# Attention and two expert layers on one core: 64-bit weights decoded with a parametric ReLU, one shift and an integer addition; every low part of the activation on VectorE

## The chip, the cores and the metric

The kernel runs on one core of a Trainium2 chip. The metric is device time in microseconds (us) of one execution. The profile is a separate execution of the same program. Engine names as in the profile: PE is TensorE's matmul (PEld its weight load), DVE is VectorE, ACT is ScalarE, POOL is GpSimd, SP is the queue that issues DMAs.

## The reference

Three stages follow one another: attention restricted to clusters, a dense layer with a rational activation (called the first layer here), and eight experts weighted by a balanced gate (the second layer).

```python
attn = softmax over k of (scale * q @ k.T where cluster(q) == cluster(k))     # B=2, H=8, S=768, D=64
x = (attn @ v), heads side by side                                            # 1536 x 512
h = x @ w_in                                                                  # w_in 512 x 2048, 64-bit floats
P = a[0] + a[1]*h + a[2]*h**2 + a[3]*h**3
Q = 1.0 + abs(b[0])*abs(h) + abs(b[1])*h**2
x = (P / (Q + 1e-6)) @ w_out                                                  # w_out 2048 x 512, 64-bit floats
gate = exp(x @ w_gate - max), rows and columns normalised 8 times             # 1536 x 8
out = sum over e of gate[:, e] * (relu(x @ w1[e]) @ w2[e])                    # w1 8 x 512 x 1024, 32-bit
```

The weights of the first layer arrive as 64-bit floats, all others as 32-bit.

## The kernel before, in words

Every matmul operand is kept as a high part (rounded for TensorE, tile names ending in h: `wh`, `hh`, `XH`) and a low part (what the rounding left: `wl`, `hl`, `XL`). A product is three matmuls: high by high, high by low, low by high (`mm3`, L784 to L786).

The first layer is cut into 8 units of 256 hidden columns. A unit has two weight pieces, `i = 0` (a slice of `w_in`) and `i = 1` (a slice of `w_out`). It is worked in 6 steps, one for each of three chunks of 512 tokens and two groups of 128 columns: 48 steps in all. In a step TensorE makes 12 matmuls for one 128x512 block of h (`stage1`) and 12 for two blocks of the output (`stage2`), four steps later.

The activation of step n is spread over the engines. ScalarE reads h from PSUM four times (`act_b`, L825 to L828), GpSimd does two multiply-adds for the numerator (L829, L830), VectorE the denominator (`act_q`, L834), ScalarE the logarithm and the exponential of its negative, which is the reciprocal (`act_r`, L838, L842). One step later VectorE makes the high part `hh` (L848), two helper values (L849, L852) and the low part `hl` (L855). In every third step from n = 6 the low part is made by GpSimd instead (L853), with a copy of the reciprocal in SBUF that a second exponential writes (L841); there are 14 such steps. VectorE also adds the output blocks to the accumulator (L887; the first unit's are copied by ScalarE, L885).

A 64-bit weight is read as two 32-bit words, `lo` and `hi`. `split_w` decodes a piece of 128x1024 weights in six pieces of work, one in each of six consecutive steps (`step_a` to `step_f`), into `wh` and `wl`: two on ScalarE (L654, L665), four on VectorE (L657, L660, L666, L667), two on GpSimd (L670, L673). There are 16 such decodings, one every three steps; those of unit 0, and the first piece of unit 1, begin while the last pair of attention heads is still at work. The 32-bit weights of the second layer take another path (`plain`, L641, L642), which is not touched.

The order on each engine is the order in which the program's loop writes the instructions (the loop from L1204); no scheduler moves them. Within a step the loop writes `act_b`, then the accumulator additions mixed with the activation's VectorE work and the pieces of decoding (L1213 to L1223), then `act_r`, `stage1`, `stage2`, and last the first piece of a new decoding. `stage1` has three PSUM buffers, so its matmuls of step n+3 wait for the last reader of h of step n, which is the low part.

Of the kernel before, what the change touches and what calls it, by code (L numbers as in the profile page):

```python
# [9 lines left out]
F32 = mybir.dt.float32  # L10
# [3 lines left out]
AF = mybir.ActivationFunctionType  # L14
ALU = mybir.AluOpType
# [15 lines left out]
def kernel(  # L31
# [15 lines left out]
    nc = tc.nc  # L47
# [69 lines left out]
    gt = nc.gpsimd.tensor_tensor  # L117
# [47 lines left out]
    lnb = const.tile([P, 2], F32, name="lnb")  # L165
# [461 lines left out]
    def split_w(ui, i):  # L627

        if (ui, i) not in staged:
            return []  # L630
        raw = staged.pop((ui, i))
        shape = [P, *wshape[i]]
        wh, wl = weights[ui, i] = (
            wp.tile(shape, F32R, tag=f"wh{i}", name=f"wh_{ui}_{i}"),
            wp.tile(shape, F32R, tag=f"wl{i}", name=f"wl_{ui}_{i}"),
        )
        if units[ui][0] == 1:

            def plain(h):
                c = slice(h * wshape[i][0] // 2, (h + 1) * wshape[i][0] // 2)  # L640
                nc.gpsimd.tensor_scalar(wh[:, c], raw[:, c], 1.0, 1.0, op0=ALU.mult, op1=ALU.mult)  # L641
                gt(wl[:, c], raw[:, c], wh[:, c].bitcast(F32), op=ALU.subtract)  # L642

            return [lambda: plain(0), lambda: plain(1)]

        lo, hi = raw[..., 0], raw[..., 1]
        mag = dp.tile(shape, F32, tag="mag", name=f"mag_{ui}_{i}")
        top = dp.tile(shape, F32, tag="top", name=f"top_{ui}_{i}")  # L650
        mi, ti = mag.bitcast(U32), top.bitcast(U32)

        def step_a():
            nc.scalar.activation(mag, hi.bitcast(F32), AF.Copy, scale=2.0 ** -112)  # L654

        def step_b():
            nc.vector.tensor_scalar(mi, mi, 3, None, op0=ALU.logical_shift_left)  # L657

        def step_c():
            nc.vector.scalar_tensor_tensor(  # L660
                ti, hi, 0x80000000, mi, op0=ALU.bitwise_and, op1=ALU.bitwise_or
            )

        def step_d():
            nc.scalar.copy(wh, top)  # L665
            nc.vector.tensor_scalar(mi, ti, 0xFF800000, None, op0=ALU.bitwise_and)  # L666
            nc.vector.scalar_tensor_tensor(mag, lo, 2.0 ** -52, mag, op0=ALU.mult, op1=ALU.mult)  # L667

        def step_e():
            gt(top, top, wh.bitcast(F32), op=ALU.subtract)  # L670

        def step_f():
            gt(wl, top, mag, op=ALU.add)  # L673

        return [step_a, step_b, step_c, step_d, step_e, step_f]

    B0, B1, B2 = 8, 14, 20
    LASTK = 2 * NT * (NPR - 1)
# [2 lines left out]
    def begin(x, ui, i):  # L681
        for y, fn in enumerate(split_w(ui, i)):
            early.setdefault(x + y, []).append(fn)

    mctx = ctx.enter_context(ExitStack())
    for kk in attention():
        if kk == LASTK:
            pctx.close()
            wp = left("wp", 2)
            stg = mctx.enter_context(tc.tile_pool(name="stg", bufs=1, reuse_waits="tile"))  # L690
            dp = mctx.enter_context(tc.tile_pool(name="dp", bufs=2, reuse_waits="tile"))
        x = kk - LASTK
        if x in (B0, B1):
            begin(x, 0, int(x == B1))
        if x == B2:
            ahead = split_w(1, 0)
            ahead.pop(0)()
        if x in (B0 + 4, B1 + 4):
            load_w(1, int(x == B1 + 4))
        for fn in early.pop(x, ()):  # L700
            fn()
# [87 lines left out]
    act = {}  # L789

    def tt(tag, n, bufs):
        return tp.tile([P, 512], F32, tag=tag, name=f"{tag}_{n}", bufs=bufs)
# [43 lines left out]
    def act_r(n):  # L836
        ps, q0 = act[n][:2]
        nc.scalar.activation(ps, q0, AF.Ln, scale=2.0 ** -LSH, bias=lnb[:, 0:1])  # L838
        if n % 3 == 0 and n > 3:
            act[n] += (tt("rr", n, 1),)  # L840
            nc.scalar.activation(act[n][-1], ps, AF.Exp, scale=-1.0, bias=lnb[:, 1:2])  # L841
        nc.scalar.activation(ps, ps, AF.Exp, scale=-1.0, bias=lnb[:, 1:2])  # L842

    def act_steps(n):
        ps, q0, _, uu, _, gh, gl, *rr = act.pop(n)
        res = tt("res", n, 2)
        return [
            lambda: nc.vector.tensor_tensor(gh, uu, ps, op=ALU.mult),  # L848
            lambda: nc.vector.scalar_tensor_tensor(  # L849
                q0, q0, GUARD, gh.bitcast(F32), op0=ALU.add, op1=ALU.mult  # L850
            ),
            lambda: nc.vector.tensor_tensor(res, uu, q0, op=ALU.subtract),  # L852
            lambda: gt(gl, res, rr[0], op=ALU.mult)  # L853
            if rr
            else nc.vector.tensor_tensor(gl, res, ps, op=ALU.mult),  # L855
        ]

    late = []
# [128 lines left out]
    def pieces_s(ui):  # L987
# [37 lines left out]
        def f():  # L1025
            st["f"] = split_w(ui, 1)
            st["f"][0]()
# [137 lines left out]
    for ui in range(NO):  # L1165
        m = units[ui][0]
        for c in range(NCH):
            for f in range(FT):
                n = ui * PER + c * FT + f
# [34 lines left out]
    for t in range(last):  # L1204
# [6 lines left out]
        outs = list(late)  # L1211
        late.clear()
        steps = [fn for n in p.get("d", ()) for fn in act_steps(n)]  # L1213
        firsts = [lambda n=n: act_q(n) for n in p.get("b", ())]
        if steps:
# [8 lines left out]
        for n in p.get("b", ()):  # L1224
            act_r(n)
# [56 lines left out]
```

## Time and profile before

| | |
|---|---|
| time, median of 3 runs | 1585.53 us (1583.32 to 1587.34) |
| the profiled execution's own time | 1586.56 us |
| its span | 1584.8 us |
| PE busy | 1536.0 us, 97% |
| DVE busy | 1200.8 us, 76% |
| POOL busy | 761.4 us, 48% |
| ACT busy | 655.6 us, 41% |

The profile counts the span from the first to the last instruction; 1.76 us of the execution lie around it. A busy PE is not PE at its peak, since matmuls overlap and their ends are modelled. The attention takes the time up to about 271 us, the first layer the time from there to about 578 us, the second layer the rest. In the rows below a window is given in us from the span's start. A step of the first layer is marked by its first ScalarE instruction (L825): step 4 begins there at 300.82, step 14 at 358.53, step 42 at 531.10 and step 47 at 557.71.

### The profile page before, as it was taken

The page shows a single profiled execution, that of the slowest core. Times are in us where ns is not written, and L with a number is a line of the kernel's source. Part 1 is how long each engine was busy: PE and PEld are TensorE (multiplying, and loading weights), DVE is VectorE, ACT ScalarE, POOL GpSimd, SP SyncE. Part 2 cuts the span into 40 slices and gives each one's busy share as a digit, 9 for nine tenths or more (in the row PEclk, how much of TensorE's full clock was granted, in tenths as well). Part 3 has the DMA queues.
Part 4 walks back from the last instruction along what each step waited for, and adds up shares of the span by engine and source line. Part 5 has one row for each costly group of instructions (what it writes and reads, how often), then busy time and mean ns, then how long its engine had stood idle before and what let it go on. Part 6 is the DMA issues. An engine that isn't in the chain of part 4 may idle for free.

```text
span 1584.8 us, 20937 instructions
## 1 busy us (share of the span) xinstructions
PE 1536.0 (97%) x7802; PEld 1351.4 (85%) x7802; DVE 1200.8 (76%) x1939; ACT 655.6 (41%) x1251; POOL 761.4 (48%) x628
## 2 busy tenths in 40 slices
PE   8999998699998999999999999999999999999999
PEld 6998997487777887898899989898999989898997
DVE  7888888999999947877766666666666666666666
ACT  5887888797777741221212122221212122121211
POOL 2343454798777894243434433453444344334420
PEclk9999999999999999999999999999999999999999
DMA  8566652111121001011101010110011011001102
GB/s 182 134 153 148 145 118 98 62 54 54 54 63 71 14 28 41 27 36 31 40 28 40 28 41 27 41 41 27 31 37 40 28 41 38 30 27 41 40 1 80
DMA packets 72726, 89.44 MB, mean 56 GB/s; under 512 B 30128, under 2 KB 50448, under 8 KB 72624
## 3 DMA queue, kind: packets, MB, share of 16 engines
q1 hardware_dynamic: 71056, 87.71, 20.0%
q8 instruction: 61, 1.00, 0.3%
q10 hardware_dynamic: 1568, 0.39, 0.1%
q14 instruction: 41, 0.34, 0.1%
HBM read 62.97 MB, written 3.19 MB: 42 GB/s over the span
## 4 chain that ended last, share of the span: by engine, by line
PE 78%; DVE 14%; issue 3%; POOL 2%; ACT 2%; DMA 1%; SPq 0%; ACTq 0%; POOLq 0%; DVEq 0%
PE y L784 12%; PE y L785 12%; PE y L786 11%; PE m L786 9%; PE m L784 9%; PE m L785 9%; PE pt L416 3%; DVE acc L887 2%; PE v L439 2%; PE v L438 2%; PE s L391 2%; PE s L392 1%; PE h L784 1%; PE h L786 1%; PE h L785 1%
## 5 line engine op out<-in xcount | busy, mean ns | idle before, releaser
L901 DVE SCALAR_TENSOR_TENSOR acc<-y,gate,acc 128x512 f32<-128x512 f32 x348 | 260.9, 750 | 177.4 <-PE y L786 176.0
L784 PE MATMUL y<-wh,gh 128*128 128x512 f32 x696 | 270.9, 389 | 1.6 <-DVE acc L901 1.6
L786 PE MATMUL y<-wh,gl 128*128 128x512 f32 x696 | 271.9, 391 | 0.0
L785 PE MATMUL y<-wl,gh 128*128 128x512 f32 x696 | 271.8, 390 | 0.0
L1018 POOL TENSOR_TENSOR rl<-sg,rh 128x512 fp32r<-128x512 f32 x29 | 45.9, 1582 | 399.9 <-ACT rh L1010 399.9
L1095 ACT COPY c<-m 128x384 f32<-128x384 f32 x58 | 27.9, 480 | 455.6 <-PE m L786 455.6
L784 PEld LDWEIGHTS y<-wh,gh 128*128 128x128 f32 x696 | 130.7, 188 | 28.3 <-DVE acc L901 2.5
L786 PEld LDWEIGHTS y<-wh,gl 128*128 128x128 f32 x696 | 130.6, 188 | 27.4
L785 PEld LDWEIGHTS y<-wl,gh 128*128 128x128 f32 x696 | 130.6, 188 | 26.1
L784 PE MATMUL h<-XH,wh 128*128 128x512 f32 x264 | 106.4, 403 | 23.1 <-DVE hl L855 23.1
L1080 DVE SCALAR_TENSOR_TENSOR gl<-v,gh 128x384 fp32r<-128x384 f32 x174 | 119.2, 685 | 0.0
L1079 ACT ACTIVATE gh<-v 128x384 fp32r<-128x384 f32 x174 | 91.1, 524 | 61.4 <-DVE v L1118 29.6
L426 DVE TENSOR_TENSOR ptl<-pt,pth 128x384 fp32r<-128x384 f32 x192 | 97.5, 549 | 23.9 <-ACT pth L425 23.0
L641 POOL TENSOR_SCALAR wh<-sg 128x512 fp32r<-128x512 f32 x70 | 43.6, 623 | 134.4 <-PE y L786 131.5
L1079 ACT ACTIVATE gh<-u 128x384 fp32r<-128x384 f32 x58 | 30.5, 526 | 184.4 <-DVE u L1104 184.4
L786 PE MATMUL h<-XH,wl 128*128 128x512 f32 x264 | 104.2, 395 | 1.1 <-POOL wl L673 1.1
L785 PE MATMUL h<-XL,wh 128*128 128x512 f32 x264 | 103.9, 394 | 0.0
L642 POOL TENSOR_TENSOR wl<-sg,wh 128x512 fp32r<-128x512 f32 x70 | 98.8, 1412 | 5.8
L425 ACT CAST pth<-pt 128x384 fp32r<-128x384 f32 x192 | 83.4, 488 | 39.7 <-PE pt L416 39.4
L397 DVE TENSOR_REDUCE nm<-s 128x1 f32<-128x768 f32 x96 | 91.2, 950 | 9.0 <-PE s L392 8.7
L416 PE MATMUL pt<-ident,pr 128*128 128x128 f32 x576 | 83.8, 278 | 7.2 <-DVE ptl L426 7.0
L405 ACT ACTIVATE pr<-s,nm 128x768 f32<-128x768 f32 x96 | 88.4, 921 | 2.5 <-DVE nm L397 2.3
(227 smaller groups left out, 4201.0 us busy)
## 6 DMA issues: line engine op xcount, KB each, us to landing
sg<-in_moe_w_dram SPq DMA_DIRECT2D x64, 512.0 KB, 3.7
stg<-in_moe_w_in_dram SPq DMA_DIRECT2D x8, 1024.0 KB, 5.5
stg<-in_moe_w_out_dram SPq DMA_DIRECT2D x8, 1024.0 KB, 4.9
st<-HQK SPq DMA_DIRECT2D x15, 384.0 KB, 3.7
qk<-in_q_dram SPq DMA_DIRECT2D x16, 192.0 KB, 3.9
vt<-in_v_dram SPq DMA_DIRECT2D x8, 384.0 KB, 5.4
rb<-rinv SPq DMA_DIRECT2D x16, 192.0 KB, 3.2
out_dram<-acc SPq DMA_DIRECT2D x12, 256.0 KB, 2.0
```

The lines of the kernel that those rows point to most:

```text
L397: nc.vector.tensor_reduce(nm, ps[:, :, :HS], axis=AX.XY, op=ALU.max, negate=True)
L405: nc.scalar.activation(pr, ps[:, :, :HS], AF.Exp, bias=nm, accum_out=rss[n][:, x : x + 1])
L416: nc.tensor.transpose(ps[:, i * P : (i + 1) * P], pv_[:, j * P : (j + 1) * P], ident)
L425: nc.scalar.copy(th[:, jj, :], ps[:, :HS])
L426: nc.vector.tensor_tensor(tl[:, jj, :], ps[:, :HS], th[:, jj, :].bitcast(F32), op=ALU.subtract)
L642: gt(wl[:, c], raw[:, c], wh[:, c].bitcast(F32), op=ALU.subtract)
L784: nc.tensor.matmul(ps, ah, bh, start=first, stop=False)
L785: nc.tensor.matmul(ps, ah, bl, start=False, stop=False)
L786: nc.tensor.matmul(ps, al, bh, start=False, stop=last)
L901: nc.vector.scalar_tensor_tensor(a, ps, p, a, op0=ALU.mult, op1=ALU.add)
L1079: nc.scalar.activation(gh[:, f], c, AF.Relu)
L1080: soon.append(lambda: nc.vector.scalar_tensor_tensor(gl[:, f], c, 0.0, gh[:, f].bitcast(F32), op0=ALU.max, op1=ALU.subtract))
```

## The change

Two edits, both in the first layer.

The decoding. `step_a` now scales the upper word with a parametric ReLU: positive values by 2^-112 as before, negative ones by a further 2^32, so that after the shift left by 3 (`step_b`, unchanged) a negative weight has its sign bit set. `step_b` also has ScalarE turn the lower word into an integer, scaled by 2^-29. `step_c` adds the two as integers, on GpSimd; the sum is the weight rounded to a 32-bit float. `step_d` copies it to `wh` on GpSimd, `step_e` takes the difference `wl` on GpSimd. Three VectorE instructions for each piece are gone (L660, L666, L667), ScalarE has two as before (the copy to `wh` gone, the conversion of the lower word new), GpSimd three in place of two, and the decoding ends one step earlier.

The activation. The second exponential into `rr` (L841) and the GpSimd product (L853) are gone; VectorE makes the low part in all 48 steps.

```diff
         def step_a():
-            nc.scalar.activation(mag, hi.bitcast(F32), AF.Copy, scale=2.0 ** -112)
+            nc.scalar.activation(mag, hi.bitcast(F32), AF.Prelu, scale=2.0 ** -112, alpha=2.0 ** 32)
 
         def step_b():
             nc.vector.tensor_scalar(mi, mi, 3, None, op0=ALU.logical_shift_left)
+            nc.scalar.activation(ti, lo, AF.Copy, scale=2.0 ** -29)
 
         def step_c():
-            nc.vector.scalar_tensor_tensor(
-                ti, hi, 0x80000000, mi, op0=ALU.bitwise_and, op1=ALU.bitwise_or
-            )
+            gt(mi, mi, ti, op=ALU.add)
 
         def step_d():
-            nc.scalar.copy(wh, top)
-            nc.vector.tensor_scalar(mi, ti, 0xFF800000, None, op0=ALU.bitwise_and)
-            nc.vector.scalar_tensor_tensor(mag, lo, 2.0 ** -52, mag, op0=ALU.mult, op1=ALU.mult)
+            nc.gpsimd.tensor_scalar(wh, mag, 1.0, 1.0, op0=ALU.mult, op1=ALU.mult)
 
         def step_e():
-            gt(top, top, wh.bitcast(F32), op=ALU.subtract)
-
-        def step_f():
-            gt(wl, top, mag, op=ALU.add)
-
-        return [step_a, step_b, step_c, step_d, step_e, step_f]
+            gt(wl, mag, wh.bitcast(F32), op=ALU.subtract)
+
+        return [step_a, step_b, step_c, step_d, step_e]
...
         nc.scalar.activation(ps, q0, AF.Ln, scale=2.0 ** -LSH, bias=lnb[:, 0:1])
-        if n % 3 == 0 and n > 3:
-            act[n] += (tt("rr", n, 1),)
-            nc.scalar.activation(act[n][-1], ps, AF.Exp, scale=-1.0, bias=lnb[:, 1:2])
         nc.scalar.activation(ps, ps, AF.Exp, scale=-1.0, bias=lnb[:, 1:2])
...
-            lambda: gt(gl, res, rr[0], op=ALU.mult)
-            if rr
-            else nc.vector.tensor_tensor(gl, res, ps, op=ALU.mult),
+            lambda: nc.vector.tensor_tensor(gl, res, ps, op=ALU.mult),
```

VectorE in the middle of the first layer, before: the rows from one step's helper value (L852) to the accumulator addition two steps on. `top` and `mag` are the decoding's tiles, `stg` holds the raw words.

```order
L852 TENSOR_TENSOR res_5062<-uu_4989,q_4991 128x512
L660 SCALAR_TENSOR_TENSOR top_1_5009<-stg_1_4850,mag_1_5008 128x1024
L855 TENSOR_TENSOR hl_1_4974<-res_5062,h_1_0_4975 128x512
L887 TENSOR_TENSOR acc<-y_0_0_5101,acc 128x512
L848 TENSOR_TENSOR hh_1_4973<-uu_5045,h_1_1_5031 128x512
L834 SCALAR_TENSOR_TENSOR q_5100<-h_22_5097,cf,q_5100 128x512
L849 SCALAR_TENSOR_TENSOR q_5047<-q_5047,hh_1_4973 128x512
L887 TENSOR_TENSOR acc<-y_0_1_5108,acc 128x512
L852 TENSOR_TENSOR res_5115<-uu_5045,q_5047 128x512
L666 TENSOR_SCALAR mag_1_5008<-top_1_5009 128x1024
L667 SCALAR_TENSOR_TENSOR mag_1_5008<-stg_1_4850,mag_1_5008 128x1024
L887 TENSOR_TENSOR acc<-y_0_2_5151,acc 128x512
```

VectorE at the same place of the changed kernel, whose line numbers are smaller (L876 is the accumulator addition, L843 the helper value, L844 the low part).

```order
L843 TENSOR_TENSOR res_5036<-uu_4962,q_4964 128x512
L844 TENSOR_TENSOR hl_1_4947<-res_5036,h_1_0_4948 128x512
L876 TENSOR_TENSOR acc<-y_0_0_5072,acc 128x512
L839 TENSOR_TENSOR hh_1_4946<-uu_5019,h_1_1_5005 128x512
L828 SCALAR_TENSOR_TENSOR q_5071<-h_22_5068,cf,q_5071 128x512
L840 SCALAR_TENSOR_TENSOR q_5021<-q_5021,hh_1_4946 128x512
L876 TENSOR_TENSOR acc<-y_0_1_5079,acc 128x512
L843 TENSOR_TENSOR res_5086<-uu_5019,q_5021 128x512
L844 TENSOR_TENSOR hl_1_4947<-res_5086,h_1_1_5005 128x512
L876 TENSOR_TENSOR acc<-y_0_2_5120,acc 128x512
```

Three instructions of 128x1024 are gone from between the helper value and the low part or the next addition, and a low part of 128x512 stands where GpSimd had it.

GpSimd over the same three steps, before.

```order
L670 TENSOR_TENSOR top_1_5009<-top_1_5009,wh_1_5006 128x1024
L829 TENSOR_TENSOR uu_5206<-uu_5206,h_24_5205 128x512
L830 TENSOR_TENSOR uu_5206<-uu_5206,ww_5207 128x512
L673 TENSOR_TENSOR wl_1_5007<-top_1_5009,mag_1_5008 128x1024
L829 TENSOR_TENSOR uu_5257<-uu_5257,h_25_5256 128x512
L830 TENSOR_TENSOR uu_5257<-uu_5257,ww_5258 128x512
L853 TENSOR_TENSOR hl_0_5191<-res_5274,rr_5240 128x512
L829 TENSOR_TENSOR uu_5309<-uu_5309,h_26_5308 128x512
L830 TENSOR_TENSOR uu_5309<-uu_5309,ww_5310 128x512
```

GpSimd over three steps of the changed kernel (L661 is the integer addition, L664 the copy to `wh`, L667 the difference).

```order
L661 TENSOR_TENSOR mag_1_4981<-mag_1_4981,top_1_4982 128x1024
L823 TENSOR_TENSOR uu_5069<-uu_5069,h_22_5068 128x512
L824 TENSOR_TENSOR uu_5069<-uu_5069,ww_5070 128x512
L664 TENSOR_SCALAR wh_1_4979<-mag_1_4981 128x1024
L823 TENSOR_TENSOR uu_5117<-uu_5117,h_23_5116 128x512
L824 TENSOR_TENSOR uu_5117<-uu_5117,ww_5118 128x512
L667 TENSOR_TENSOR wl_1_4980<-mag_1_4981,wh_1_4979 128x1024
L823 TENSOR_TENSOR uu_5176<-uu_5176,h_24_5175 128x512
L824 TENSOR_TENSOR uu_5176<-uu_5176,ww_5177 128x512
```

Each of the three steps has one decoding instruction behind its two numerator instructions; before, one of the three had the activation's product.

## Rows read from the trace of the kernel before

**Rows 1.** Busy time by stretch: span, length, engines, clock, DMA share, GB/s.
```profile
core 0: us, PE busy (x) PEld busy (x) DVE busy (x) ACT busy (x) POOL busy (x), PEclk, DMA share, GB/s
246.00:300.82 54.82, 40.09 (x198) 33.67 (x197) 48.25 (x63) 39.86 (x72) 34.37 (x25) 0.91 0.19 60
300.82:358.53 57.71, 54.37 (x232) 42.83 (x232) 56.22 (x70) 52.42 (x84) 53.65 (x31) 1.00 0.18 62
358.53:531.10 172.57, 159.16 (x674) 125.96 (x673) 172.03 (x224) 127.11 (x195) 136.25 (x86) 0.99 0.17 56
531.10:557.71 26.61, 26.61 (x119) 22.00 (x118) 21.81 (x35) 21.04 (x35) 22.61 (x18) 1.00 0.07 21
```

**Rows 2.** The same stretches, L825 alone: its count is the number of steps.
```profile
300.82:358.53 57.71, 5.93 (x10) 1.00 0.18 62
358.53:531.10 172.57, 16.60 (x28) 0.99 0.17 56
531.10:557.71 26.61, 2.98 (x5) 1.00 0.07 21
```

**Rows 3.** Chain that ended last, 408 to 427 us: start, length, what.
```profile
408.20 0.86 DVE top L660
...
409.84 0.68 DVE hl L855
...
414.16 0.62 DVE mag L666
...
415.03 1.90 issue
416.93 0.68 DVE acc L887
...
426.68 0.86 DVE top L660
```

**Rows 4.** Groups by line: busy us, mean ns | idle before, releaser.
```profile
L829 POOL TENSOR_TENSOR uu<-uu,h 128x512 f32<-128x512 f32 x48 | 67.5, 1407 | 37.1 <-ACT uu L827 37.1
L830 POOL TENSOR_TENSOR uu<-uu,ww 128x512 f32<-128x512 f32 x48 | 66.0, 1376 | 3.8
...
L641 POOL TENSOR_SCALAR wh<-sg 128x512 fp32r<-128x512 f32 x70 | 43.6, 623 | 134.4 <-PE y L786 131.5 <-PE h L785 2.9
...
L673 POOL TENSOR_TENSOR wl<-top,mag 128x1024 fp32r<-128x1024 f32 x16 | 39.7, 2480 | 0.2
L670 POOL TENSOR_TENSOR top<-top,wh 128x1024 f32<-128x1024 f32 x16 | 39.3, 2454 | 0.1
...
L654 ACT ACTIVATE mag<-stg 128x1024 f32<-128x1024 f32 x16 | 18.4, 1150 | 1.6 <-POOL wl L673 1.6
...
L665 ACT CAST wh<-top 128x1024 fp32r<-128x1024 f32 x16 | 17.2, 1076 | 2.1 <-DVE top L660 2.1
...
L145 ACT ACT_TABLE_LOAD x1 | 1.3, 1283 | 2.1 <-issue 2.1
```

**Rows 5.** The shift's line by itself: shortest, median, longest in ns.
```profile
L657 DVE TENSOR_SCALAR mag<-mag x16: 680/1856/1870, 253.1 to 513.0; 128x1024 uint32<-128x1024 uint32 x16
```

**Rows 6.** Chain that ended last, 246 to 300 us.
```profile
255.86 1.47 DVE top L660
...
259.13 0.61 DVE mag L666
...
259.77 1.23 DVE mag L667
...
270.77 1.14 DVE top L660
...
271.94 0.71 DVE mag L666
...
272.67 0.83 DVE mag L667
...
293.98 1.76 DVE mag L666
```

More of the change, by code (lines that the diff above doesn't have):

```diff
@@ L838, in act_r @@
         nc.scalar.activation(ps, q0, AF.Ln, scale=2.0 ** -LSH, bias=lnb[:, 0:1])
-        if n % 3 == 0 and n > 3:
-            act[n] += (tt("rr", n, 1),)
-            nc.scalar.activation(act[n][-1], ps, AF.Exp, scale=-1.0, bias=lnb[:, 1:2])
         nc.scalar.activation(ps, ps, AF.Exp, scale=-1.0, bias=lnb[:, 1:2])
     def act_steps(n):
-        ps, q0, _, uu, _, gh, gl, *rr = act.pop(n)
+        ps, q0, _, uu, _, gh, gl = act.pop(n)
         res = tt("res", n, 2)
```

## The prediction

> **What bounds the kernel now.** Read first the busy time by stretch [rows 1]. From 358.53 to 531.10 us, where 28 steps of the first layer run [rows 2], VectorE is busy 172.03 of 172.57 us, TensorE 159.16 and less than that in truth, since its records overlap. Behind it, from 531.10 to 557.71, where no decoding is left for VectorE, TensorE is busy the whole 26.61 us and VectorE 21.81. So the same loop has two limits: 172.57/28 = 6.163 us a step while VectorE decodes, 26.61/5 = 5.322 us a step when TensorE is alone the limit. The chain that ended last says the same: between 408 and 427 us it is VectorE from one end to the other, and in it stand L660, L666 and L667, the three decoding instructions that the change takes away [rows 3]. The reader is to see there too that "issue" stands beside them: VectorE was waiting in the middle of an instruction, for something that the profile does not name.
>
> The first ten steps that have output blocks, from 300.82 to 358.53, take 5.771 us each [rows 1, 2]. There the first unit's blocks are copied by ScalarE, VectorE has less to do and POOL is at 53.65 of 57.71 us. Before 300.82 TensorE is busy 40.09 of 54.82 us: the last attention heads, the first decodings and the empty pipeline of the first layer.
>
> Outside 246 to 558 us nothing is edited, so the sum is made for this stretch alone. It is made against the profiled execution's own 1586.56 us (span 1584.8 us); the median of the runs is 1.03 us below it, which is within what the runs differ.
>
> **VectorE's new load.** One decoding falls in three steps: from one L660 (408.20) to the next (426.68) are 18.48 us [rows 3]. L660 holds VectorE from 408.20 to 409.84, 1.64 us; L666 and L667 together from 414.16 to 416.93, 2.77 us. These 4.41 us go. What comes is one low part in three steps, 0.68 us by L855's row there. 18.48 - 4.41 + 0.68 = 14.75 us, or 4.92 a step, against TensorE's 5.32.
>
> **POOL's new load.** Two numerator instructions a step, 1.407 + 1.376 us [rows 4], make 8.35 in three steps. The product (L853) goes. The difference `wl` stays with L673's 2.480. The copy to `wh` is new on POOL at this size: L641 does the same on 128x512 in 0.623 us, so 0.62 at least and 1.25 at most; I take 1.25. The integer addition is in no row. From below it is bounded by that 1.25 (one input in place of two). The nearest row from above is the float addition of the same shape, L670 with 2.454, and I take this; what it costs if integers are slower is a rival. Sum 8.35 + 2.454 + 1.25 + 2.480 = 14.53 us, 4.84 a step, where POOL has 136.25/28 = 4.87 now [rows 1]. It is the same load, spread more evenly: one decoding instruction in each step.
>
> **ScalarE's new load.** It loses the copy L665 (1.076 us) and gains the conversion of the lower word; its nearest row is L654, which reads the other word of the same tile in 1.150 us, and a conversion could lie anywhere from L665's 1.076 up. That is +0.07 in three steps on 127.11/28 = 4.54 a step [rows 1, 4]; the second exponential that goes is not even counted. Prelu in place of Copy I take at L654's own duration.
>
> So no engine has more than 4.92 us a step, and TensorE's 5.32 becomes the limit. Will it be reached? Between 531.10 and 557.71 TensorE held it with POOL at 85% and VectorE at 82% [rows 1]. Now VectorE would be at 92% of 5.32, POOL at 91%. Both queues are in order, and `hl` of a step must be done before `stage1` three steps later, so some of the small delays will reach TensorE. I take 5.45, nearer to 5.32 than to the 5.77 of the stretch from 300.82, where POOL had 93%.
>
> The terms:
> - 28 steps: 28 x (6.163 - 5.45) = 20.0 us. Ends: 23.5 (at 5.322) and 11.0 (at 5.771).
> - 10 steps from 300.82: 10 x (5.771 - 5.45) = 3.2 us. Ends: 4.5 and 0.
> - Before 300.82. On the chain stand 1.47 + 0.61 + 1.23 us of the first decoding, 1.14 + 0.71 + 0.83 of the second and 1.76 of the third [rows 6], 7.75 us in all. They do not all come back: ScalarE now has the conversion in the queue one step ahead of where it had the copy, and the last heads' additions on POOL stand behind the integer addition. Ends: 7.75, and a loss of 2.45 if one POOL addition of L670's length comes late into the end of attention with nothing gained for it. I take 5.5, since the chain names these VectorE instructions one behind the other.
> - The last five steps: TensorE is the limit before and after, 0. The removal of L853 and L841 there is hidden by TensorE.
>
> Sum 20.0 + 3.2 + 5.5 = 28.7; 1586.56 - 28.7 = 1557.9, so 1558 us. The favourable ends give 35.8 (1551), the unfavourable 8.5 (1578).
>
> **A rule to be weighed against this.** The shift L657 stays on VectorE. Its row has 680 ns as the shortest and 1856 as the median [rows 5]: in most cases it waits 1.18 us inside the instruction, a little less than one POOL numerator instruction lasts. The Trainium skill, "SBUF — State Buffer", section "Who interferes with whom", says that a VectorE instruction in a two-port mode and a GpSimd instruction take the same pair of ports for the whole instruction, and that the second one blocks fully. The trace agrees with it by this one row. What the rule makes of the new order is the first rival below.
>
> **Rivals.**
>
> *The shift blocked behind longer POOL work.* POOL now has a 2.4 us decoding instruction in two steps of three, and the shift of a piece is written in the same step as the difference `wl` of the piece before. If it waits that whole instruction, it takes 0.68 + 2.48 = 3.16 us in place of the row's 1.86: VectorE then needs 14.75 - 1.86 + 3.16 = 16.05 us for three steps, 5.35 each, and in that one step it has 4.3 + 3.2 us to do. `hl` comes late there, TensorE waits, and the pace is that of the crowded stretch, 5.77. For it: rows 5. Against it: the other two steps have room to catch up. Time: 11.0 + 0 + 3 = 14 us less, 1572.
>
> *Integer addition slow on POOL* (the other side). If integers go another way through GpSimd than floats, POOL becomes the limit. It decides from 18.48 - 8.35 - 1.25 - 2.48 = 6.40 us for one addition, 2.6 times L670. At four times, 9.8 us, three steps need 21.9 us, 7.29 a step: 28 x 1.13 + 10 x 1.52 = 47 us more, 1633. For it: no row has an integer operation on POOL. Against it: POOL's two-input rows go by size alone (1.4 us for 512, 2.45 for 1024) [rows 4]. The Trainium skill, "GPSIMD Engine Reference", section 4.1, says that the cores add 32-bit integers natively; no run shows it yet.
>
> *Prelu needs another table.* L145 loads ScalarE's table once, in 1.283 us, for all functions before [rows 4]. If Prelu were not in it, each of 16 decodings would load twice: 2 x 1.283/3 = 0.86 us a step, ScalarE at 5.4 of 5.45, and with its place ahead of the next step's four reads of h the pace would again be 5.77 at best: 1572 or more. Against it: the instruction order of the changed kernel has no further table load. The Trainium skill, "ScalarE: Activation LUTs", section "Table sets", lists cheap functions that stand in every set, and Prelu is not among those that it names.
>
> *No change.* TensorE gains, but late conversions, additions and copies at the front of the layer give it back; a POOL addition near 6 us would do it: within 5 us of 1586.
>
> **How the numbers follow.** Forecast 0.74 (own range 1551 to 1570), shift blocked 0.13, Prelu's table 0.03, no change 0.03, slow addition 0.07. The first three are faster by over 0.3% (some 5 us, about what a measurement here can tell from no change): 0.90; same 0.03; slower 0.07. The range for 8 in 10 takes the forecast's band, widened below by 3 us for the steps' pace and the start coming out well together, and reaches over the blocked shift: 1548 to 1576.
>
> **What would show it.** In the profile after: 24 matmuls in about 5.4 us through the 28 steps, TensorE without gaps and VectorE at 90% in place of 99.7%; the integer addition near 2.45 us and the copy near 1.2; one table load; the conversion near 1.15 us on ScalarE; step 4 about 5 us earlier, step 42 about 29 us earlier, and the same distance kept to the end. Wrong if the shift takes over 3 us and the low parts then hold `stage1`, if POOL is at 99%, or if step 4 is not earlier, in which case the start's term is the failed one.

## The result, and the profile after

| | before | after |
|---|---|---|
| median | 1586.43 us (1583.32 to 1587.54, 4 runs) | 1562.47 us (1562.08 to 1563.26, 4 runs) |
| ratio to before | 1 | 0.9853, 95% interval 0.9836 to 0.987 |
| the profiled execution | 1586.56 us, span 1584.8 us | 1562.66 us, span 1560.9 us |
| VectorE busy | 1200.8 us | 1149.3 us |

The profiled execution is 23.9 us shorter; 28.7 had been forecast. First the busy time by stretch, as in [rows 1], cut at the same steps (4, 14, 42 and 47). Columns: stretch, its length, then each engine's busy time and count, granted clock, DMA share, GB/s.

```profile
core 0: us, PE busy (x) PEld busy (x) DVE busy (x) ACT busy (x) POOL busy (x), PEclk, DMA share, GB/s
246.00:294.11 48.11, 39.68 (x191) 32.61 (x190) 35.79 (x50) 39.21 (x70) 35.35 (x27) 0.93 0.30 97
294.11:349.13 55.02, 50.99 (x223) 41.25 (x222) 42.30 (x62) 50.09 (x81) 50.50 (x33) 1.00 0.18 58
349.13:507.04 157.91, 154.88 (x673) 125.23 (x672) 146.40 (x206) 122.80 (x186) 127.22 (x84) 1.00 0.16 54
507.04:534.46 27.42, 27.42 (x123) 22.70 (x122) 22.34 (x36) 20.17 (x32) 18.52 (x16) 1.00 0.06 20
```

Against [rows 1], the part before step 4 is 54.82 - 48.11 = 6.7 us shorter, the ten steps 57.71 - 55.02 = 2.7, the 28 steps 172.57 - 157.91 = 14.7, the last five 0.8 longer (their start before was marked late, as told below), and the rest behind them 0.65 shorter. VectorE is no longer full (146.40 of 157.91 us, 93%), and TensorE is nearly so: 154.88. The pace of the 28 steps is 157.91/28 = 5.640 us.

Not all of the 6.7 us is the change's. The 89th of the attention's 96 exponentials runs before any edited instruction (the first is L654, at 249.77 us before and 247.51 after); its row, before and after:

```profile
242.42 0.92 ACT L405 ACTIVATE pr<-s,nm 128x768 f32<-128x768 f32 x1
240.17 0.92 ACT L405 ACTIVATE pr<-s,nm 128x768 f32<-128x768 f32 x1
```

Already there the profiled execution of before was 2.25 us behind. In the nine profiled executions of this document this row starts anywhere from 239.10 to 243.01 us; what makes the difference was not followed. Counted from it, step 4 comes 4.5 us earlier by the change, and step 47 comes 21.0 us earlier. The interval of the ratio stands for 20.6 to 26.0 us of gain and holds this as well as the 23.9.

The instructions that the prediction had no row for, each line by itself (shortest, median, longest in ns; first and last start; form). L657 answers to [rows 5]; L661 is the integer addition, L664 the copy to `wh`, L667 the difference, L654 the parametric ReLU, L658 the conversion of the lower word.

```profile
L657 DVE TENSOR_SCALAR mag<-mag x16: 682/2782/2812, 250.9 to 489.6; 128x1024 uint32<-128x1024 uint32 x16
...
L661 POOL TENSOR_TENSOR mag<-mag,top x16: 2368/2405/2427, 255.0 to 494.9; 128x1024 uint32<-128x1024 uint32 x16
...
L664 POOL TENSOR_SCALAR wh<-mag x16: 1046/1058/1080, 257.5 to 500.8; 128x1024 fp32r<-128x1024 f32 x16
...
L667 POOL TENSOR_TENSOR wl<-mag,wh x16: 2353/2400/2842, 260.3 to 506.2; 128x1024 fp32r<-128x1024 f32 x16
...
L654 ACT ACTIVATE mag<-stg x16: 1114/1159/1178, 247.5 to 483.9; 128x1024 f32<-128x1024 f32 x16
...
L658 ACT ACTIVATE top<-stg x16: 1132/1156/1218, 251.2 to 487.3; 128x1024 uint32<-128x1024 uint32 x16
```

The shift apart, all came near or below what was taken: the integer addition costs what the float difference beside it costs. The shift is the exception: its median went from 1.86 to 2.78 us, though it is the same instruction. Where it stands shows why. In order of time, VectorE in one step (start, length, engine, line):

```profile
404.16 0.68 DVE L843 TENSOR_TENSOR res<-uu,q 128x512 f32<-128x512 f32 x1
404.75 2.78 DVE L657 TENSOR_SCALAR mag<-mag 128x1024 uint32<-128x1024 uint32 x1
407.46 0.67 DVE L844 TENSOR_TENSOR hl<-res,h 128x512 fp32r<-128x512 f32 x1
```

and GpSimd over the same time:

```profile
404.59 2.40 POOL L667 TENSOR_TENSOR wl<-mag,wh 128x1024 fp32r<-128x1024 f32 x1
407.17 1.51 POOL L823 TENSOR_TENSOR uu<-uu,h 128x512 f32<-128x512 f32 x1 [0.19 <-ACT uu L821]
```

The difference `wl` starts 0.16 us ahead of the shift; the shift ends 0.54 us after it, and only then comes the low part. In the kernel before, the shift met a difference of the same length, but began 1.09 us behind its start:

```profile
402.09 1.87 DVE L657 TENSOR_SCALAR mag<-mag 128x1024 uint32<-128x1024 uint32 x1
401.00 2.41 POOL L670 TENSOR_TENSOR top<-top,wh 128x1024 f32<-128x1024 f32 x1
```

It ended 0.55 us after that one. So the meeting is not new; what is new is that the shift begins almost together with the difference and waits for nearly the whole of it. The chain that ended last shows who waits for that (start, length, what):

```profile
404.84 1.74 DVE mag L657
406.57 0.88 issue
407.46 0.69 DVE hl L844
408.19 0.50 PE h L778
408.69 0.24 PE h L779
```

TensorE's next `stage1` begins when the low part at 407.46 has freed its PSUM buffer. The waits of steps 14 to 42 name this release nine times, once for each blocked shift (us in total, times, longest):

```profile
PEld h L778 <- DVE hl L844: 6.8, 9, 0.8
PE h L778 <- DVE hl L844: 3.0, 9, 0.4
```

From here on to 418 us the chain is TensorE; then it goes through VectorE and the next shift again.

### The profile page after: what moved, and what is told of

The parts are those of the page before. It is cut to its first block, busy times and chain, and to the rows that moved or that the text cites. A ratio compares the mean times of both kernels' runs of the same rounds, so it can differ in the third digit from the quotient of the medians.

```text
span 1560.9 us, 20895 instructions
## 1 busy us (share of the span) xinstructions
PE 1529.5 (98%) x7802; PEld 1350.1 (86%) x7802; DVE 1149.3 (74%) x1905; ACT 649.3 (42%) x1237; POOL 746.9 (48%) x630
## 4 chain that ended last, share of the span: by engine, by line
PE 87%; DVE 7%; ACT 2%; issue 2%; DMA 1%; POOL 0%; SPq 0%; ACTq 0%; DVEq 0%; POOLq 0%
PE y L780 13%; PE y L779 13%; PE y L778 13%; PE m L780 9%; PE m L778 9%; PE m L779 9%; PE pt L416 4%; PE h L778 3%; PE h L780 3%; PE h L779 3%; PE v L438 2%; PE v L439 2%; PE s L391 2%; PE s L392 2%; DVE mag L657 1%
```

## The experiments

Times are medians, ratios are to the kernel before in the same job. "After" stands for the changed kernel. Expectations are quoted as they were written before the runs.

**1. The shift behind the low part.**

```diff
-            steps = outs[:1] + [a] + firsts + [b] + outs[1:] + [c] + p.get("w", []) + [d]
+            steps = outs[:1] + [a] + firsts + [b] + outs[1:] + [c, d] + p.get("w", [])
```

> The changed kernel, with the pieces of decoding (the shift among them) written behind the low part in each step, not ahead of it. Theory (the shift waits 2.1 us for GpSimd's difference to end, and the low part behind it is late for the PSUM buffer of the step three later): the low part is no longer late, TensorE loses its 0.66 us in three steps, the pace of the 28 steps falls from 5.640 to 5.44 to 5.50 us, the time by 4 to 6 us from 1562.5 to about 1557. Rival (VectorE as a whole is too full in that step, wherever the shift stands): the wait passes to the next step's first instructions, and the time is within 1.5 us of 1562.5.

1554.26 us (1553.56 to 1555.35), ratio 0.9802 (0.9788 to 0.9817). The profile by stretch, for steps 14 to 42 and 42 to 47:

```profile
346.24:498.31 152.07, 152.07 (x673) 125.92 (x672) 140.68 (x206) 122.67 (x187) 127.49 (x85) 1.00 0.17 56
498.31:525.72 27.41, 27.41 (x123) 22.69 (x122) 22.33 (x36) 20.15 (x32) 18.48 (x16) 1.00 0.06 20
```

TensorE has no gap left, 152.07 of 152.07 us, and the pace is 5.431 us. The shift is still blocked, though for less long, as its line shows:

```profile
L657 DVE TENSOR_SCALAR mag<-mag x16: 682/2054/2209, 249.8 to 482.2; 128x1024 uint32<-128x1024 uint32 x16
```

but what stands behind it now (the accumulator addition of the next step) has time. The theory holds: not VectorE's amount of work, but the low part behind the blocked shift kept TensorE waiting. The 28 steps gave 157.91 - 152.07 = 5.8 us. The whole gain of some 8 us is more than was expected; 2.9 us of it lie before step 14, which begins at 346.24 in place of 349.13. Of those, 2.0 lie in steps 4 to 13, where two of three shifts were blocked (2.81 and 1.57 us). The 0.9 before step 4 is not the edit's: the exponential that started at 240.17 us in the changed kernel starts at 239.10 here. Counted from it to step 42, the edit is worth 266.87 - 259.21 = 7.7 us.

**2. An empty step between the shift and the addition.**

```diff
-        return [step_a, step_b, step_c, step_d, step_e]
+        return [step_a, step_b, lambda: None, step_c, step_d, step_e]
```

> The changed kernel, with an empty step between the shift and the integer addition, so that a piece's shift falls in the step in which GpSimd copies the piece before to its high part (1.06 us) and not in the one in which it takes the difference (2.40 us). No instruction is added or removed. Theory (the shift waits for the whole of whatever GpSimd instruction began before it): the shift's median falls from 2.78 to 1.3 to 1.8 us, the low part is 1.0 to 1.4 us earlier, the time is about 1558. Rival (the loss comes from VectorE's amount of work or from ScalarE's conversion, not from the meeting with GpSimd): time within 1.5 us of 1562.5, and the wait for the low part stays near 0.5 us in three steps.

1556.47 us (1554.79 to 1557.76), ratio 0.9815 (0.98 to 0.983). The shift's line, and the 28 steps:

```profile
L657 DVE TENSOR_SCALAR mag<-mag x16: 682/1405/1430, 249.9 to 482.3; 128x1024 uint32<-128x1024 uint32 x16
```

```profile
347.04:499.14 152.10, 152.10 (x673) 125.94 (x672) 133.97 (x206) 123.29 (x186) 126.88 (x85) 1.00 0.17 56
```

One shift of this run, and the copy to `wh` that it meets:

```profile
400.74 1.41 DVE L657 TENSOR_SCALAR mag<-mag 128x1024 uint32<-128x1024 uint32 x1
400.55 1.05 POOL L664 TENSOR_SCALAR wh<-mag 128x1024 fp32r<-128x1024 f32 x1
```

The shift now meets GpSimd's copy of 1.06 us and lasts 1.4 us in place of 2.8; 12.4 us of VectorE's busy time are gone from the stretch (146.40 to 133.97) with the same 206 instructions. So the shift's length is set by what is left of the GpSimd instruction that it meets. TensorE is again without a gap.

**3. Shift and addition as one VectorE instruction.** The lower word's three bits are cut off, not rounded, and joined by "or".

```diff
-            nc.vector.tensor_scalar(mi, mi, 3, None, op0=ALU.logical_shift_left)
-            nc.scalar.activation(ti, lo, AF.Copy, scale=2.0 ** -29)
+            nc.scalar.activation(ti, lo, AF.Copy, scale=2.0 ** -29, bias=-0.5)
...
-            gt(mi, mi, ti, op=ALU.add)
+            nc.vector.scalar_tensor_tensor(
+                mi, mi, 3, ti, op0=ALU.logical_shift_left, op1=ALU.bitwise_or
+            )
```

> The changed kernel with the shift and the integer addition in one VectorE instruction (shift left by 3, or with the lower word's top three bits), so that the lower word's part is cut off where the addition rounded it. GpSimd loses 2.4 us in three steps, VectorE loses the shift (2.78 with its wait) and gains an instruction with two inputs in SBUF that took 1.2 to 1.8 us in the kernel before. Theory of the blocked shift: VectorE's part falls to 4.7 us a step, the instruction stands in a step where GpSimd has only the numerator, the pace goes to 5.44 to 5.50, time about 1557. Rival (any VectorE instruction that shares GpSimd's port blocks as long): the instruction takes 2.5 us or more, the pace stays near 5.64, time 1560 to 1564.

1556.19 us (1554.71 to 1557.53), ratio 0.9814 (0.9799 to 0.9828). The line, and the 28 steps:

```profile
L660 DVE SCALAR_TENSOR_TENSOR mag<-mag,top x16: 1216/1217/1592, 253.8 to 487.7; 128x1024 uint32<-128x1024 uint32 x16
```

```profile
347.01:499.09 152.08, 152.08 (x673) 125.92 (x672) 132.78 (x206) 123.54 (x186) 103.87 (x75) 1.00 0.17 56
```

The instruction stands in a step in which GpSimd has only the numerator, and it runs between two numerators:

```profile
404.47 1.29 POOL L825 TENSOR_TENSOR uu<-uu,ww 128x512 f32<-128x512 f32 x1
406.13 1.22 DVE L660 SCALAR_TENSOR_TENSOR mag<-mag,top 128x1024 uint32<-128x1024 uint32 x1
408.53 1.30 POOL L824 TENSOR_TENSOR uu<-uu,h 128x512 f32<-128x512 f32 x1 [2.77 <-ACT uu L822]
```

It meets no GpSimd instruction, so the rival, that such an instruction is blocked as long, was not put to the test here. GpSimd has 103.87 us in place of 127.22, and the time of the stretch is the same as in experiments 1 and 2: GpSimd's load was not a limit.

**4 and 5. Each edit alone.** Experiment 4 is the kernel before with the new decoding, experiment 5 the kernel before with every low part on VectorE. Their edits are the two halves of the change's diff.

> The kernel before with the new decoding alone; in 14 of 48 steps the low part is still GpSimd's product, with the second exponential. By the sum, VectorE loses 0.68 us in three steps against the changed kernel, GpSimd gains 1.3 to 1.7 and is at 5.1 us a step, ScalarE gains 0.69. If the decoding brought all of the gain and the other edit is neutral: 1562 to 1564. If the product on GpSimd now lengthens the shift's wait and the chain of the low part: 1566 to 1572. If VectorE's load still counts: 1558 to 1560.

> The kernel before with the other edit alone: the old decoding, every low part on VectorE. VectorE is the limit in the 28 steps, so by its load the pace rises by 0.60 to 0.68 us in three steps: 28 x 0.2 = 6 us, about 1591. Rival (the product that leaves GpSimd also takes away waits of the decoding's VectorE instructions for the port): the pace stays within 0.05 us of 6.16 and the time within 2 us of before.

Decoding alone: 1563.65 us (1562.49 to 1563.94), ratio 0.9862 (0.9845 to 0.9878), the whole gain of the change within what is measured. Its shift is blocked as in the changed kernel (median 2.74 us), and from the attention's exponential to step 42 both take 266.87 us. The other edit alone: 1584.48 us (1582.75 to 1587.01), ratio 0.9996 (0.9987 to 1.0006): no change, where I had expected 6 us more. The time fits the rival; its pace does not quite, 6.067 us where it had 6.16 within 0.05. The 28 steps are shorter than before, the ten steps ahead of them longer (59.14 us against 57.71, not followed further). The instruction that came to VectorE was paid by one that got shorter. L667 before:

```profile
L667 DVE SCALAR_TENSOR_TENSOR mag<-stg,mag x16: 1224/2198/2206, 259.8 to 525.7; 128x1024 f32<-128x1024 uint32 x16
```

and in experiment 5:

```profile
L667 DVE SCALAR_TENSOR_TENSOR mag<-stg,mag x16: 1224/1225/2206, 260.3 to 525.3; 128x1024 f32<-128x1024 uint32 x16
```

In GpSimd's order of time in experiment 5, nothing runs while L667 does (415.46 to 416.69), where the product had been:

```profile
411.81 1.29 POOL L830 TENSOR_TENSOR uu<-uu,ww 128x512 f32<-128x512 f32 x1
417.35 1.29 POOL L829 TENSOR_TENSOR uu<-uu,h 128x512 f32<-128x512 f32 x1 [4.25 <-ACT uu L827]
```

The 0.97 us that this median lost cover the 0.68 us of the low part; the shift took back part of it (its median went from 1.86 to 2.07 us). From step 19 on three steps take 7.00 + 5.06 + 6.24 = 18.30 us, where they took 18.48.

**6 and 7. Two edits together.** Experiment 6 joins the edits of 1 and 3, experiment 7 those of 1 and 2.

> The changed kernel with two of the earlier edits together: shift and addition in one VectorE instruction, and the pieces of decoding behind the low part. Each of them alone brought the 28 steps to 5.43 us. Theory (24 matmuls at 0.227 us, 5.44 us a step, are now the limit): together they bring no more in those steps, 5.43 again, and the time is 1553 to 1557. Rival (the pace was still held by VectorE or GpSimd): the pace falls below 5.40 and the time to 1550 or less.

> The changed kernel with the empty step between shift and addition and the pieces of decoding behind the low part. The 28 steps stay at 5.43 us. At the front the empty step had brought step 0 to 269.93 us, 2.6 earlier than in the changed kernel, and lost 2.8 at step 5, where weights of the second unit come a step later. If these add up as they stood: 1554 to 1557. If the late weights of step 5 were due to the shift blocked there: 1551 to 1553.

1557.17 us (1554.49 to 1558.62), ratio 0.9826 (0.9812 to 0.9839), and 1555.01 us (1554.72 to 1558.55), ratio 0.9819 (0.9805 to 0.9832). In experiment 6 the 28 steps go from 348.87 to 500.89 us, in experiment 7 from 347.01 to 499.11: 152.0 and 152.1 again. Two cures of the same wait bring no more than one, though the shift of experiment 7 is hardly blocked any more (median 0.70 us); 24 matmuls a step are the limit now. In experiment 7 step 4 begins at 292.50 and step 5 only at 300.97, 8.47 us later, as in experiment 2 (292.53 and 301.00), so that loss at the front comes with the empty step and not with a blocked shift. What exactly is late there was not followed further.

Experiment 1 is the fastest measured, 8 us below the changed kernel; its interval overlaps those of the other four with a cure (2, 3, 6, 7), and lies clear of the changed kernel's. From the attention's exponential to step 42 the five take 259.2, 260.0, 259.6, 259.6 and 260.0 us. Experiment 6 is the slowest of them by its median, a little above its forecast; in its profile the attention was already 2.2 us later than in experiment 1 (241.26 against 239.10).

## Why the prediction was right, and where it was off

- **VectorE as the limit before, TensorE after.** Right in the main: the decoding alone gave the whole gain, and TensorE was busy 154.88 of 157.91 us. In every third step the chain still runs through VectorE and its shift (until 408.19 in the rows above), and that is the first rival's mechanism. So the steps hold part of both, and the measured 1562.5 us lies between the forecast's 1558 and the rival's 1572. The forecast's band (1551 to 1570) was wide enough to take both, so that the time fell into it does not by itself show which mechanism ran; the experiments do.
- **The three new costs.** The integer addition (2.405 us against 2.454 taken), the conversion (1.156 against 1.150) and Prelu (1.159 against 1.150) were right; the copy was 1.058 where 1.25 was taken. ScalarE has no further table load: the groups after show none but L145's. Both rivals that rested on an unknown price fall.
- **The pace of the 28 steps: the term that was mis-sized**, 20.0 us forecast, 14.7 measured (13.9 without the late mark at 531.10, below). The step that failed is the one that let "some of the small delays" reach TensorE and took 5.45 us a step; it was 5.640. Experiments 1 to 3 show what came in its place. Without the late low part the stretch lasts 152.07 us, 172.57 - 152.07 = 20.5 us less than before (19.7 without that mark), so 5.45 was the pace of a kernel in which no delay reaches TensorE, and **the blocked shift** took 5.8 us of it. It had been given 0.13 as a rival. Its mechanism was told rightly (the shift meets the difference of the piece before; 2.78 us where 3.16 were worked out); its price was too high (14 us of gain left in all, where 23.9 came). The steps take 6.13, 5.65 and 5.19 us in turn, 16.97 for three, so that TensorE loses 0.65 us against three of its own 5.44; the rival had 17.3, and it gave the ten steps 0 and the start 3, where 2.7 and 4.5 came. The reading of [rows 5] beside it was wrong: the 1.18 us were no numerator instruction's, they were the rest of the 2.41 us difference L670, as the two rows of before above show, and a 2.4 us decoding instruction stood in two steps of three before as well.
- **The floor** of 5.322 us was misread. The stretch from 531.10 to 557.71 [rows 1] was cut at ScalarE's first instruction of a step, which was late at 531.10; in TensorE's own order of time the `stage1` groups begin 5.44 us apart there (532.45, 537.92, 543.36), and experiments 1 to 3 have 5.43 with TensorE full. The value taken, 5.45, lies close to TensorE's own 5.44 all the same; the favourable end, 23.5, could not be had.
- **The ten steps**: 3.2 forecast, 2.7 measured. **The start**: 5.5 forecast, 6.7 measured, of which 2.25 were there before any edited instruction ran; 4.5 are left for the change. So each of the three terms fell short, and the attention's 2.25 us brought the profile's 23.9 nearer to 28.7 than the terms did: that part was luck. The chain of [rows 6] had 7.75 us of VectorE's decoding. From the attention's exponential to step 4 it is 58.40 us before, 58.39 in experiment 5, 54.35 in experiment 4 and 53.94 after, so the start's gain is the decoding's. What is late next there is no decoding instruction on VectorE but the reciprocal sums' DMA, the last heads' products and, as the prediction had warned, pieces of decoding on ScalarE, as the chain of the changed kernel shows:

```profile
251.30 1.04 ACT top L658
...
267.04 3.33 DMA rb<-rinv
...
270.49 0.87 DVE x1f L492
...
271.39 1.07 DVE XH L493
...
272.49 2.64 DVE XL L494
275.13 1.59 DVE x1f L492
...
287.92 1.20 ACT top L658
```

- **The sum of VectorE's load** was 4.92 us a step forecast, 146.40/28 = 5.23 measured: the 0.31 are the longer shift, (2.78 - 1.86)/3. Counting the removed instructions at their length of before and adding the low part's 0.68 was right here. In experiment 5, where L667 stays, the same count failed, since L667 is shorter without GpSimd's product.

## What to carry to other kernels

When work moves from VectorE to GpSimd, look up which VectorE instructions last longer at some places than at others (shortest and median of their line) and which GpSimd instructions they will now meet. Here such an instruction waited for the rest of the GpSimd instruction that it met, so its length was set by when both begin, not by the amount of work. Put it behind the one that others wait for; here that one line was worth 7.7 us of 1562. Compare profiles from a mark ahead of the first edited instruction; here 2.25 of 23.9 us lay before it. Read a floor from the engine that makes it (distance of its own groups), not from a marker on another engine.

## What the runs showed of the hardware

A 128x1024 shift on VectorE takes 0.68 us alone, 1.4 where it meets a 1.06 us GpSimd copy, and 2.78 where it meets a 2.40 us GpSimd difference. In the 28 steps of the kernel before, of the changed kernel and of experiments 1 and 2, it ends 0.54 to 0.56 us after the GpSimd instruction that it met, whether 0.86, 1.3, 1.5 or 2.25 us of that were left. The Trainium skill, "SBUF — State Buffer", section "Who interferes with whom", says that a VectorE instruction in a two-port mode and a GpSimd instruction lock the same ports, and that whichever comes second blocks until the first has ended. These lengths agree with it; the mode in which the shift ran is not in the profile. An instruction with two SBUF inputs behaves alike: L667 took 2.20 us in the kernel before, with GpSimd's product beside it, and 1.22 in experiment 5, without. A 32-bit integer addition on GpSimd took 2.405 us for 128x1024, a float difference 2.400. The Trainium skill, "GPSIMD Engine Reference", section 4.1, says that the cores add integers natively; the equal times agree with it.
